# Two lone token tiles taken as one pair by seven block products, and a new order of all instructions

## The chip, the cores and the metric

The kernel runs on one core of one Trainium2 chip. The metric is device time in microseconds, the median of several runs; less is better. TensorE (PE) multiplies, VectorE (DVE) and ScalarE (ACT) evict its results and do the elementwise work, GpSimd (POOL) issues the loads, SyncE (SP) issues the transposes by DMA and most stores.

## The reference

An attention with squared relu is followed by a mixer of tokens and channels. With 8 batches, 12 heads, 448 positions and a head size of 64:

```
def _attn_ref(q, k, v) -> np.ndarray:
    S = q.shape[2]
    scale = 1.0 / np.sqrt(q.shape[-1])
    scores = scale * np.matmul(q, k.transpose(0, 1, 3, 2))
    attn = np.maximum(scores, 0.0) ** 2 / S
    return np.matmul(attn, v).astype(np.float32)

def _moe_ref(x, w_tok1, w_tok2, w_ch1, w_ch2) -> np.ndarray:
    xt = x.transpose(0, 2, 1)
    h = np.maximum(xt @ w_tok1, 0.0) @ w_tok2
    u = x + h.transpose(0, 2, 1)
    h2 = np.maximum(u @ w_ch1, 0.0) @ w_ch2
    return (u + h2).astype(np.float32)
```

x is the attention's output with the heads side by side (8 x 448 x 768); w_tok1 is 448 x 256, w_tok2 256 x 448, w_ch1 768 x 1536, w_ch2 1536 x 768. Inputs and output are float32; the kernel multiplies in bfloat16.

## The kernel before

The work is cut into 24 sets of four heads (three sets for a batch). In the words of the order table, with s a set, c one of seven chunks of positions, b a batch and p a pair of batches:

- `ld` loads q, k or v of a set (POOL). `T` transposes q and k on PE for the first ten sets, and `cp` copies the result; later sets are cast (`iq`, `ik`) and transposed by DMA on SP (`xq`, `xk`).
- `S` is a score step of four matmuls in 64*64 tiles; `r` (two of them) is its relu on ACT or DVE, `q` the square. `V` is a value step of four matmuls in 64*64 tiles, `xe` its eviction.
- `X` or, from set 6 on, `xd` (a DMA transpose on SP) turns x; `t1` and `t2` are the token products, `rt` and `u` their evictions; `ub` transposes u by DMA on SP.
- `C1` is the first channel product of a batch; from the third batch on `fast1` makes it of seven block products (`M1`, a 2 x 2 scheme with fewer multiplications) with `tu`, `s1`, `d1` and `y1` as sums and evictions.
- The second channel product takes token tiles of 128. A pair of batches has 896 tokens, seven tiles. `fast2` takes two tiles by seven block products (`M2`, six matmuls of 384 columns each, with `h` as sums and `d2` as evictions); `channel2` takes a tile alone in two halves of twelve matmuls (`C2`, one sum `h....s`, evictions `c2e`). With seven tiles there are three pairs and one lone tile in each pair of batches, four lone tiles in all: `ALONE = [2, 6, 2, 4]`. The very last tile that is finished, tile 4 of the fourth pair, is a lone one and is evicted and stored in three parts.
- `w1` and `w2` are sums of the weights, `st` stores an output tile, `fill` writes matmuls whose result nobody reads.

Nothing is scheduled by the compiler: `ORDER` is a table of words, written out by a planner beforehand, and `Order.run` issues the words one after another. Each engine works through its own in this order. A word also names the PSUM banks, or the engine (`:A` is ACT, `:D` is DVE), or for a load the transfer behind which it is held. The lines that matter below are, before the change: L343 and L345 relu, L355 and L357 square, L472 transposes of q and k, L497 and L566 and L610 the DMA transposes of k and q, of x and of u, L515 scores, L542 values, L688 sums, L713 and L722 a lone tile's matmuls and evictions, L780 the `M1` and L847 the `M2` products, L860 and L862 the evictions of `M2`, L970 filling matmuls. In the changed kernel the same lines stand one to four numbers lower down.

Of the kernel before, what the change touches and what calls it, by code (L numbers as in the profile page):

```python
# [22 lines left out]
ALONE = [2, 6, 2, 4]  # L23
TILES = [7 * p + t for p, order in enumerate(((0, 1, 2, 3, 4, 5, 6), (4, 5, 6, 0, 1, 2, 3), (0, 1, 2, 3, 4, 5, 6), (5, 6, 0, 1, 2, 3, 4))) for t in order]
# [49 lines left out]
ldf.0 ldf.1 ldk0.0 ldk0.1 ident ldk1.0 ldv2.0 cast0.0:D cast0.1:A ldq1.0 ldk1.1 cast1.0:D cast1.1:A ldq1.1  # L74
T0.0:0 ldv0.1 T0.1:1 cp0.0:D ldv0.0 cp0.1:D ldq2.0 ldk2.0 fill:4*5 S0.3:23
S0.1:45 S0.6:67 r0.3.0:A r0.3.1:D ldq2.1 S0.5:01 r0.1.0:A r0.1.1:D S0.0:23 wt1.1 r0.6.0:A r0.6.1:D r0.0.0:A
ldv1.1 q0.1:D r0.0.1:A ldk2.1 q0.3:D r0.5.0:A T1.0:45 r0.5.1:A q0.0:D S0.4:67 ldq3.0 S0.2:23 cp1.0:A cp1.1:D
ldk3.0 q0.5:D V0.0:01 r0.2.0:A S1.2:54 V0.1 q0.6:D r0.2.1:A ldv1.0 r0.4.0:A r0.4.1:D S1.3:23 ldv2.1 r1.2.0:A
q0.2:D r1.2.1:A wt1.0 q0.4:D r1.3.0:A V0.2 S1.1:67 ldv3.0 V0.3 q1.2:D r1.3.1:A V0.4 S1.4:54 r1.1.0:A ldk4.1
r1.1.1:D S1.0:23 r1.4.0:A r1.4.1:D ldk3.1 S1.6:67 r1.0.0:A V0.5 V0.6 q1.1:D r1.0.1:A ldk4.0 xe0.1:D xe0.0:A  # L80
ldq3.1 r1.6.0:A T2.0:54 q1.0:D r1.6.1:A q1.3:D X0.0:2 wt2 X0.1:3 cp2.0:A cp2.1:D S1.5:01 V1.0:67 ldq5.0 V1.1
q1.4:D r1.5.0:A V1.2 S2.3:45 ldq4.1 V1.3 r1.5.1:A xc0.0:D V1.4 xc0.1:D r2.3.0:A ldk5.1 S2.0:02 q1.5:D r2.3.1:A
S2.2:13 ldv4.0 q1.6:D r2.0.0:A fill:4*3 V1.5 S2.1:45 r2.0.1:A r2.2.0:D ldq6.1 r2.1.0:A r2.1.1:D S2.6:02 V1.6
ldv3.1 r2.2.1:A t1.0.0:1 q2.0:D xe1.0:A ldq5.1 S2.4:45 xe1.1:D r2.6.0:A V2.0:36 r2.6.1:A q2.1:D X1.1:0 ldq4.0
rt0.0:A q2.2:D r2.4.0:A fill:7*2 V2.1 S2.5:72 ldk6.0 q2.3:D r2.4.1:A V2.2 T3.0:14 r2.5.0:A xc1.1:D ldv5.0 V2.3
q2.4:D r2.5.1:A t2.0.0:5 cp3.0:A ldk5.0 cp3.1:D t1.1.1:0 X1.0:7 u0.0:D wc1.0 rt1.1:A V2.4 S3.2:24 xc1.0:A
q2.5:D t2.1.1:1 r3.2.0:A q2.6:D ldq6.0 S3.1:50 r3.2.1:A u1.1:D S3.4:72 ldk6.1 V2.5 r3.1.0:A V2.6 q3.2:D ub0.3
t1.1.0:4 r3.1.1:A ldv4.1 xe2.1:D xe2.0:A S3.0:15 wc1.2 t1.0.1:0 r3.4.0:A r3.4.1:D X2.1:6 rt1.0:A q3.1:D X2.0:3
r3.0.0:A wc2.0 S3.3:72 xc2.1:D rt0.1:A r3.0.1:A T4.0:41 xc2.0:D wc1.1 q3.4:D r3.3.0:A S3.6:60 t2.0.1:3
r3.3.1:A cp4.0:D t1.2.1:5 wc2.2 r3.6.0:A u0.1:D S3.5:72 r3.6.1:A cp4.1:D t1.2.0:4 rt2.1:A t2.1.0:6 r3.5.0:A  # L90
q3.0:D t2.2.1:3 rt2.0:A q3.3:D r3.5.1:A S4.1:05 S4.4:17 u1.0:D r4.1.0:A V3.0:42 V3.1 u2.1:D r4.1.1:A ub0.2
S4.3:60 V3.2 r4.4.0:A q3.5:D V3.3 S4.0:53 r4.4.1:A V3.4 r4.3.0:D ldk7.0 t2.2.0:1 r4.3.1:A ub0.5 q3.6:D V3.5
r4.0.0:A T5.0:76 u2.0:D r4.0.1:A ldq7.0 S4.2:05 V3.6 q4.1:D cp5.0:A ub0.4 C1.0.3:1 ldk7.1 xe3.1:D xe3.0:A
cp5.1:D ldv5.1 r4.2.0:A C1.0.1a:3 q4.0:D r4.2.1:A c1e0.3:A q4.3:D S4.6:72 S4.5:46 V4.0:05 q4.2:D r4.6.0:A V4.1
C1.0.1 r4.5.0:A r4.5.1:D C1.0.2a:1 r4.6.1:A q4.4:D c1e0.1:A C1.0.2 q4.5:D T6.0:74 q4.6:D c1e0.2:A S5.5:62 V4.2
cp6.0:A cp6.1:D V4.3 V4.4 ldq7.1 V4.5 r5.5.0:D S5.3:31 r5.5.1:A V4.6 S6.3:47 r5.3.0:A r5.3.1:D X3.0:6 xe4.0:A
xe4.1:D C1.0.9:2 r6.3.0:A r6.3.1:D xc3.0:A q5.3:D C1.0.10:3 q5.5:D c1e0.9:A q6.3:D wc2.1 X4.0:1 c1e0.10:A
# [24 lines left out]
q9.1:A ub1.1 V8.4 V8.5 ldk14.0:xk11 ik12:D S9.3:51 V8.6 r9.6.1:D C1.1.11:7 xe8.0:A q9.2:D xe8.1:A r9.3.1:A
r9.6.0:D C1.1.8:4 xd8 r9.3.0:A ldk13.0:st1.0 r9.5.1:A ldq13.0:st1.0 q9.3:A t2.6.1:6 q9.5:D ub1.3 C1.1.7:3
q9.6:D c1e1.11:A u6.1:D c1e1.8:A t2.7.0:1 ub1.4 c1e1.7:D V9.0:05 V9.1 u7.0:D S10.1:27 V9.2 V9.3 r10.1.1:A
h0.3.0:D S10.5:46 st2.64 V9.4 r10.1.0:A V9.5 r10.5.0:D V9.6 st0.0 S11.0:31 S10.4:72 xe9.1:A xe9.0:D M2.0.3.2:4
xk12 r10.4.1:A r10.5.1:D r11.0.1:A r11.0.0:D t2.7.1:5 r10.4.0:A d2.0.3.11a:D S10.0:02 xd9 S10.6:61 h0.3.1:D
S10.3:37 r10.0.0:A M2.0.3.5:4 u7.1:D r10.0.1:A ldk14.1:ub1.4 q11.0:A r10.6.0:D xq12 M2.0.3.1:0 ldv10.1:st2.64
iq13:D r10.3.1:A ik13:D r10.3.0:A M2.0.5.2:2 ub2.0 d2.0.3.11b:D r10.6.1:A h0.5.0:D S11.1:56 h0.3.2:D S10.2:73
t1.8.0:1 r10.2.1:A xk13 h0.3.3:D r11.1.0:A r10.2.0:D M2.0.3.6 rt8.0:A d2.0.5.11a:D ub2.2 r11.1.1:A q10.0:D
t2.8.0:3 q10.4:A d2.0.3.12a:D M2.0.5.1:5 d2.0.3.22a:D ub2.1 ldv11.1:xq12 u8.0:D S11.2:71 t2.8.1:2 ldq14.0  # L130
r11.2.0:A M2.0.3.3 r11.2.1:A u8.1:D ldv10.0:xq12 xq13 q10.2:A h0.5.1:D ldq14.1 t1.9.0:6 d2.0.5.11b:D q10.1:A
ldv11.0:xq12 tu2.2:D S11.3:37 ldk16.1:xk13 ik14:D S11.4:12 r11.3.1:A M2.0.3.7 h0.5.2:D ldv12.1:ub2.2 q11.2:A
r11.4.0:D ldq16.1:xk13 M2.0.5.6 r11.4.1:A d2.0.3.22b:D ldk16.0:ub2.1 r11.3.0:A h0.5.3:D M2.0.5.5:7 rt9.0:A
d2.0.5.12a:D q10.3:A ldq15.1 M2.0.3.4 d2.0.5.22a:D q11.4:A q11.1:D ldk15.1 M2.0.5.3 d2.0.3.12b:D q10.6:A
# [111 lines left out]
def kernel(ctx: ExitStack, tc: tile.TileContext, q: bass.AP, k: bass.AP, v: bass.AP, moe_w_tok1: bass.AP, moe_w_tok2: bass.AP, moe_w_ch1: bass.AP, moe_w_ch2: bass.AP, out: bass.AP):  # L246
# [506 lines left out]
    def fast1(b):  # L753
# [17 lines left out]
        for e in range(0, EC // 2, 2):  # L771
# [54 lines left out]
            for j in range(2):  # L826
                c1e[b, e + j] = [c11, c12]
                c1e[b, 6 + e + j] = [c22, y]

    def fast2(p, t, q):  # L830
        r2 = r2s[p]
        (s1, s2, s4), free = sum_set(p)
        out1, parts, store1 = stores(p, t)
# [19 lines left out]
        def take(name, n, cols, u, deps, first):  # L853
# [10 lines left out]
            if first:  # L864
                read_u.setdefault((p, n), []).append(o)
# [138 lines left out]
```

## Time and profile before

| | |
|---|---|
| three runs | 345.43, 346.44, 347.01 us, median 346.44 |
| the profiled execution | 345.03 us, its span 343.2 us |
| granted clock, mean over the span | 0.993 |
| DMA traffic | 50.19 MB, mean 146 GB/s |
| loads of q, k, v (142 of 112 KB) | 4.6 to 4.7 us median to landing |
| six loads of channel weights (768 KB) | 16.9 us median to landing |
| stores of a half tile at the end (96 KB) | 2.1 to 2.4 us median to landing |

The span runs from the first to the last instruction of the profiled execution. Times in rows of the profile are us unless marked ns. A row of the groups gives line, engine, operation, output <- inputs, shapes, count, then busy us and mean ns of one, then the idle time before. A row of the chain of waits gives start, us, and the work, with the number of matmuls.

### The profile page before, as it was taken

Reading aid. Unit: us, or ns where it says so; the run is one execution under the profiler, and the core shown is the slowest. Engines: PE = TensorE matmul, PEld = TensorE weight load, DVE = VectorE, ACT = ScalarE, POOL = GpSimd, SP = SyncE. Lnnn points to the kernel's source line nnn. Section 1 sums busy time; section 2 is a strip of 40 time slices with the busy share of each in tenths; the row PEclk is TensorE's granted clock in tenths of the full one; section 3 lists DMA queues with packets and bytes.
Section 4 is the critical chain, followed back from the end, with each engine's and each line's share of the span. In section 5 each row is a group of like instructions: output and inputs, shape, how many; then the busy total and the mean of one; then the engine's idle time right before and its main releaser. Section 6 shows DMA issues by size and latency. Waiting matters only on the chain.

```text
span 343.2 us, 9395 instructions
## 1 busy us (share of the span) xinstructions
PE 334.0 (97%) x3792; PEld 217.5 (63%) x3792; DVE 296.7 (86%) x577; ACT 242.5 (71%) x456; POOL 91.8 (27%) x157
## 2 busy tenths in 40 slices
PE   7799999999999999999999999999999999999995
PEld 3456455555555557675777655786579787787762
DVE  4999998799988999899979999899897886877763
ACT  3999986868998797999799986978974633031000
POOL 8986211383221371222811233200002000000000
PEclk9899999999999999999999999999999999999999
DMA  8999999798999999999999999996459032241464
GB/s 139 188 188 180 154 183 207 122 168 130 173 178 133 217 158 159 205 173 182 169 189 173 178 157 217 155 186 130 80 112 129 19 79 32 48 114 38 109 160 139
DMA packets 98939, 50.19 MB, mean 146 GB/s; under 512 B 71568, under 2 KB 95952, under 8 KB 98896
## 3 DMA queue, kind: packets, MB, share of 16 engines
q1 hardware_dynamic: 72736, 26.92, 45.3%
q0 software_dynamic: 25136, 21.47, 45.2%
q10 hardware_dynamic: 1024, 1.21, 1.2%
q8 instruction: 29, 0.48, 0.6%
q14 instruction: 14, 0.11, 0.1%
HBM read 43.38 MB, written 11.01 MB: 159 GB/s over the span
## 4 chain that ended last, share of the span: by engine, by line
PE 89%; DMA 3%; DVE 3%; SPq 3%; issue 0%; DVEq 0%; POOLq 0%
PE m_ps L847 24%; PE m_ps L780 22%; PE sc_ps L515 10%; PE acc_ps L542 9%; PE m_ps L623 6%; PE t_ps L588 6%; PE h_ps L597 5%; PE m_ps L713 5%; DMA u_sb<-uT 2%; SPq L610 2%; PE kqT_ps L472 1%; DVE arena L357 1%; DMA arena<-in_k_dram 1%; SPq L497 1%; PE x_ps L579 1%; DVE arena L345 1%
## 5 line engine op out<-in xcount | busy, mean ns | idle before, releaser
L343 ACT ACTIVATE arena<-sc_ps 128x448 bf16<-128x448 f32 x238 | 117.3, 570 | 14.8 <-PE sc_ps L515 13.4
L345 DVE TENSOR_SCALAR arena<-sc_ps 128x448 bf16<-128x448 f32 x98 | 59.4, 619 | 5.1 <-PE sc_ps L515 3.1
L357 DVE TENSOR_TENSOR arena<-arena 128x896 bf16<-128x896 bf16 x105 | 62.0, 620 | 1.0 <-ACT arena L343 0.9
L355 ACT ACTIVATE arena<-arena 128x896 bf16<-128x896 bf16 x63 | 58.5, 960 | 0.1
L371 POOL DMA_DIRECT2D arena<-in_v_dram x48 | 29.2, 618 | 98.0 <-PE m_ps L780 20.2
L515 PE MATMUL sc_ps<-arena 64*64 64x448 bf16 x672 | 54.2, 362 | 0.4
L542 PE MATMUL acc_ps<-arena 64*64 64x448 bf16 x672 | 46.4, 358 | 1.7 <-DVE arena L357 1.6
L780 PEld LDWEIGHTS <-wc 128*128 128x128 bf16 x432 | 40.8, 98 | 6.1 <-issue 3.2
L371 POOL DMA_DIRECT2D arena<-in_q_dram x46 | 28.1, 618 | 44.6 <-DMA u_sb<-uT 8.0
L371 POOL DMA_DIRECT2D arena<-in_k_dram x48 | 29.5, 620 | 21.2 <-DMA out_dram<-out_sb 9.4
L780 PEld LDWEIGHTS <-ws 128*128 128x128 bf16 x324 | 30.5, 98 | 4.5 <-issue 2.5
L515 PEld LDWEIGHTS <-arena 64*64 64x64 bf16 x672 | 19.7, 106 | 20.5 <-issue 13.6
L601 DVE TENSOR_TENSOR uT<-h_ps,xT 128x448 bf16<-128x448 f32 x48 | 29.1, 619 | 1.7 <-PE h_ps L597 1.5
L847 PE MATMUL m_ps<-wc,r 128*128 128x384 bf16 x162 | 30.3, 327 | 0.0
L542 PEld LDWEIGHTS <-arena 64*64 64x64 bf16 x672 | 20.6, 108 | 15.3 <-issue 5.3
L623 PE MATMUL m_ps<-uT,wc 128*128 128x448 bf16 x144 | 30.1, 353 | 0.0
L847 PEld LDWEIGHTS <-r 128*128 128x128 bf16 x216 | 20.2, 98 | 15.1 <-issue 3.1
L793 ACT ACTIVATE arena<-m_ps 128x448 f32<-128x448 f32 x18 | 9.4, 545 | 24.7 <-PE m_ps L780 7.6
L597 PE MATMUL h_ps<-wt,r_sb 128*128 128x448 bf16 x96 | 25.4, 353 | 0.0
L588 PE MATMUL t_ps<-x_sb,wt 128*128 128x256 bf16 (+1 forms) x216 | 25.4, 261 | 0.0
L780 PE MATMUL m_ps<-uT,wc 128*128 128x224 bf16 x216 | 25.0, 259 | 0.0
L847 PEld LDWEIGHTS <-sums 128*128 128x128 bf16 x180 | 17.3, 98 | 12.0 <-issue 1.3
(86 smaller groups left out, 507.2 us busy)
## 6 DMA issues: line engine op xcount, KB each, us to landing
out_dram<-out_sb SPq DMA_DIRECT2D x42, 192.0 KB, 3.7
arena<-in_k_dram POOLq DMA_DIRECT2D x48, 112.0 KB, 4.6
arena<-in_v_dram POOLq DMA_DIRECT2D x48, 112.0 KB, 4.6
arena<-in_q_dram POOLq DMA_DIRECT2D x46, 112.0 KB, 4.7
wc<-in_moe_w_ch_dram POOLq DMA_DIRECT2D x6, 768.0 KB, 16.9
out_dram<-arena SPq DMA_DIRECT2D x4, 192.0 KB, 2.8
out_dram<-out_sb ACTq DMA_DIRECT2D x8, 96.0 KB, 2.4
out_dram<-out_sb SPq DMA_DIRECT2D x8, 96.0 KB, 2.1
```

The source lines that it names most:

```text
L343: nc.scalar.activation(out, ps, AF.Relu)
L345: nc.vector.tensor_scalar(out=out, in0=ps, scalar1=0.0, scalar2=None, op0=ALU.max)
L355: nc.scalar.activation(x, x, AF.Square)
L357: nc.vector.tensor_tensor(out=x, in0=x, in1=x, op=ALU.mult)
L371: o.ins = nc.gpsimd.dma_start(out=raws[t][s % NR][64 * half:64 * (half + 1)], in_=src[b, h0:h0 + 2].rearrange('e (p c) d -> p e (c d)', c=KC))
L515: nc.tensor.matmul(o.ps[e][64 * half:64 * (half + 1), :S], lhsT=lhsT, rhs=rhs, start=True, stop=True, skip_group_check=True)
L542: nc.tensor.matmul(o.ps[half][64 * e:64 * (e + 1), :S], lhsT=r[rows, e, c * D:(c + 1) * D], rhs=sq[rows, e, :], start=c == 0, stop=c == KC ...
L588: nc.tensor.matmul(o.ps[:, j, :], lhsT=wt1[:, c, j * 128:(j + 1) * 128], rhs=x_sb[:, p0:p1, c, :], start=c == 0, stop=c == 3)
L597: nc.tensor.matmul(o.ps[:, :S], lhsT=r1[:, j, a * 128:(a + 1) * 128], rhs=wt2[:, j, :], start=j == 0, stop=j == JC - 1)
L623: nc.tensor.matmul(ps[:, :S], lhsT=wc1[:, g, e * 128:(e + 1) * 128], rhs=uT[:, g, off:off + S], start=g == 0, stop=g == CC - 1)
L780: nc.tensor.matmul(o.ps[:, j * HB:(j + 1) * HB], lhsT=lhs[:, g, (e + j) * 128:(e + j + 1) * 128], rhs=rhs[:, g], start=j == g == 0 and not ...
L847: nc.tensor.matmul(o.ps[:, :HN], lhsT=lhs[:, e], rhs=rhs[:, e], start=e == 0 and not on, stop=e == EC // 2 - 1, skip_group_check=True)
```

## The change

The third pair's lone tile 2 and the fourth pair's lone tile 4 now form a pair of `fast2`, whose two tiles may lie in different pairs of batches. It is made with the last batch. `ALONE` loses its last two entries, the order in which output tiles take their buffers follows, and the lone tiles left are those of the first two pairs. A dependency of the first `fast1` on the weights' load is stated as well. `ORDER` is written anew from the first word to the last, as a planner made it that serves transfers in the order of their issue.

```
-ALONE = [2, 6, 2, 4]
-TILES = [7 * p + t for p, order in enumerate(((0, 1, 2, 3, 4, 5, 6), (4, 5, 6, 0, 1, 2, 3), (0, 1, 2, 3, 4, 5, 6), (5, 6, 0, 1, 2, 3, 4))) for t in order]
+ALONE = [2, 6, None, None]
+LONE = ((2, 2), (3, 4))
+TILES = [7 * p + t for p, order in enumerate(((0, 1, 2, 3, 4, 5, 6), (4, 5, 6, 0, 1, 2, 3), (0, 1, 3, 4, 5, 6), (5, 6))) for t in order] + [21, 22, 16, 25, 23, 24]
...
-ldf.0 ldf.1 ldk0.0 ldk0.1 ident ldk1.0 ldv2.0 cast0.0:D cast0.1:A ldq1.0 ldk1.1 cast1.0:D cast1.1:A ldq1.1
-T0.0:0 ldv0.1 T0.1:1 cp0.0:D ldv0.0 cp0.1:D ldq2.0 ldk2.0 fill:4*5 S0.3:23
+ldf.0 ldf.1 cast1.0:A ldk0.0 ldk0.1 ldq1.1 ldk1.1 ident ldq1.0 cast0.0:D ldq2.0 cast0.1:D fill:1*8 T0.0:0
+cp0.0:A ldk1.0 cast1.1:D ldk2.1 ldv0.1 T0.1:2 cp0.1:D fill:4*8 ldq2.1 ldv0.0 S0.1:35 S0.2:67 S0.0:14 r0.1.0:A
...
-    order = [k % NO for k in range(3 * NT)] + [4, 5, 0, 1, 2, 3, 4]
+    order = [k % NO for k in range(3 * NT - 1)] + [4, 5, 0, 1, 2, 3, 4, 5]
...
+            w1 = list(wc1_ops.values()) if b == FIRST1 else []
-            m1 = product('1', A(0, 0), u11, every + ([got[e - 2, '5']] if e else []))
-            m2 = product('2', A(1, 0), u21, every)
+            m1 = product('1', A(0, 0), u11, every + w1 + ([got[e - 2, '5']] if e else []))
+            m2 = product('2', A(1, 0), u21, every + w1)
...
-    def fast2(p, t, q):
-        r2 = r2s[p]
-        (s1, s2, s4), free = sum_set(p)
+    def fast2(p, t, q, p2=None):
+        p2 = p if p2 is None else p2
+        (s1, s2, s4), free = sum_set(max(p, p2))
         out1, parts, store1 = stores(p, t)
-        out2, parts, store2 = stores(p, q)
+        out2, parts, store2 = stores(p2, q)
...
-        h11, h12, h21, h22 = (r2[:, e:e + 6, c] for c in (te, to) for e in (0, 6))
-        ce, co = (tokens(p, t), tokens(p, q))
+        r2, r2q = (r2s[p], r2s[p2])
+        h11, h12, h21, h22 = (r[:, e:e + 6, c] for r, c in ((r2, te), (r2q, to)) for e in (0, 6))
+        ce, co = (tokens(p, t), tokens(p2, q))
...
-                first, then = ([x for x in PAIRS[p] if x[0] in whole(p, b % 2)], [ALONE[p]] if b % 2 else [])
+                first, then = ([x for x in PAIRS[p] if x[0] in whole(p, b % 2)], [])
+            if b == 2 * B // 2 - 1:
+                fast2(*LONE[0], LONE[1][1], LONE[1][0])
```

Three places show what the new table moves. The first is on PE, around the first score of set 7 (`S7.3`, here sc_ps_1564 and sc_ps_1565 before, sc_ps_1544 and sc_ps_1545 now). Before:

```order
L847 LDWEIGHTS r2_75
L847 MATMUL m2_ps_1551<-wc2_68,r2_75 128x384
L515 LDWEIGHTS arena_69
L515 MATMUL sc_ps_1564<-arena_69 64x448
L515 LDWEIGHTS arena_69
L515 MATMUL sc_ps_1565<-arena_69 64x448
L515 LDWEIGHTS arena_69
L515 MATMUL sc_ps_1564<-arena_69 64x448
L515 LDWEIGHTS arena_69
L515 MATMUL sc_ps_1565<-arena_69 64x448
L579 LDWEIGHTS xT_64
L579 MATMUL x_ps_1571<-ident_63,xT_64 128x128
```

Now:

```order
L543 LDWEIGHTS arena_69
L543 MATMUL acc_ps_1510<-arena_69 64x448
L516 LDWEIGHTS arena_69
L516 MATMUL sc_ps_1544<-arena_69 64x448
L516 LDWEIGHTS arena_69
L516 MATMUL sc_ps_1545<-arena_69 64x448
L516 LDWEIGHTS arena_69
L516 MATMUL sc_ps_1544<-arena_69 64x448
L516 LDWEIGHTS arena_69
L516 MATMUL sc_ps_1545<-arena_69 64x448
L516 LDWEIGHTS arena_69
L516 MATMUL sc_ps_1550<-arena_69 64x448
```

The score stood alone between a product of the second channel step and a transpose of x, both of 128 rows; now it stands between the last value step of set 5 and another score of set 7, all of 64 rows.

The second place is on SP, behind the first six transposes of u (L610, now L611): the transposes of u for the second batch (128x4x128), of k and q for set 10 (`arena`), of x for sets 6 and 7 (x_sb0, x_sb1), and stores of the first output tiles. Before:

```order
L610 DMA_TRANSPOSE u_sb_74<-uT_73 128x3x128 x6
L497 DMA_TRANSPOSE arena_69<-arena_69 128x7x128
L566 DMA_TRANSPOSE x_sb0_70<-xT_64 128x8x128
L668 DMA out_0_dram<-out_sb1_79 64x768
L497 DMA_TRANSPOSE arena_69<-arena_69 128x7x128
L668 DMA out_0_dram<-out_sb2_80 64x768
L566 DMA_TRANSPOSE x_sb1_71<-xT_64 128x8x128
```

Now:

```order
L611 DMA_TRANSPOSE u_sb_74<-uT_73 128x3x128 x6
L611 DMA_TRANSPOSE u_sb_74<-uT_73 128x4x128
L669 DMA out_0_dram<-out_sb1_79 64x768
L611 DMA_TRANSPOSE u_sb_74<-uT_73 128x4x128
L669 DMA out_0_dram<-out_sb1_79 64x768
L611 DMA_TRANSPOSE u_sb_74<-uT_73 128x4x128
L669 DMA out_0_dram<-out_sb0_78 64x768
L669 DMA out_0_dram<-out_sb2_80 64x768
L567 DMA_TRANSPOSE x_sb0_70<-xT_64 128x8x128
L567 DMA_TRANSPOSE x_sb1_71<-xT_64 128x8x128
L498 DMA_TRANSPOSE arena_69<-arena_69 128x7x128 x2
```

Three transposes of u and four stores moved ahead of the first transposes of x, the two of x stand one directly behind the other, and those of set 10 came behind them.

The third place is the end on DVE, where the last lone tile was evicted in three parts (L722, in arena). Before:

```order
L722 TENSOR_TENSOR arena_69<-m2_ps_5674,arena_69 128x128
L688 TENSOR_TENSOR arena_69<-arena_69 128x768
L860 TENSOR_TENSOR arena_69<-arena_69,m2_ps_5461 128x384
L722 TENSOR_TENSOR arena_69<-m2_ps_5649,arena_69 128x256
L688 TENSOR_TENSOR arena_69<-arena_69 128x6x128
L688 TENSOR_TENSOR arena_69<-arena_69 128x768
L688 TENSOR_TENSOR arena_69<-arena_69 128x6x128
L860 TENSOR_TENSOR out_sb0_78<-arena_69,m2_ps_5718 128x384
L860 TENSOR_TENSOR out_sb2_80<-arena_69,m2_ps_5688 128x384
L862 TENSOR_TENSOR out_sb0_78<-out_sb0_78,m2_ps_5726 128x384
L722 TENSOR_TENSOR arena_69<-m2_ps_5699,arena_69 128x384
```

Now the last rows are:

```order
L864 TENSOR_TENSOR out_sb2_80<-u_sb_74,m2_ps_5596 128x384
L864 TENSOR_TENSOR out_sb1_79<-arena_69,m2_ps_5735 128x384
L866 TENSOR_TENSOR out_sb2_80<-out_sb2_80,m2_ps_5554 128x384
L866 TENSOR_TENSOR out_sb1_79<-out_sb1_79,m2_ps_5683 128x384
L864 TENSOR_TENSOR arena_69<-arena_69,m2_ps_5647 128x384
L864 TENSOR_TENSOR arena_69<-arena_69,m2_ps_5655 128x384
L866 TENSOR_TENSOR out_sb3_81<-out_sb3_81,m2_ps_5596 128x384
L866 TENSOR_TENSOR arena_69<-arena_69,m2_ps_5647 128x384
L866 TENSOR_TENSOR arena_69<-arena_69,m2_ps_5655 128x384
L864 TENSOR_TENSOR out_sb3_81<-arena_69,m2_ps_5596 128x384
L864 TENSOR_TENSOR arena_69<-arena_69,m2_ps_5655 128x384
L864 TENSOR_TENSOR out_sb1_79<-arena_69,m2_ps_5683 128x384
```

The parts of a lone tile are gone from the end; evictions of four pairs of tiles stand there interleaved, those of the new pair (out_sb2 from u_sb, and out_sb3) among them.

More of the change, by code (lines that the diff above doesn't have):

```diff
@@ new lines @@
+r11.4.1:A ub2.4 ik14:D M2.0.5.4 tu2.0:D r11.4.0:A xe10.1:D r12.1.1:A ldq16.1:xk13 xe10.0:A xk14 S12.2:62
+tu2.1:D S12.0:73 s1.2.0.1:A w1.2.0:D M1.2.0.5:1 r12.0.0:A q11.0:D t2.9.1:0 r12.0.1:A ub2.3 ldk16.1:xk13
+d2.0.5.21:D s1.2.0.5:A q11.4:D M1.2.0.2:7 xd10 M1.2.0.6 r12.2.0:A u9.1:D r12.2.1:A M1.2.0.3 q11.6:A
+d1.2.0.11:D S12.5:35 iq14:D V11.0:62 S12.3:07 r12.5.0:D st5.64 V11.1 V11.2 s1.2.0.2:A r12.3.0:A d1.2.0.12:D
+V11.3 V11.4 st4.0 r12.3.1:A V11.5 V11.6 iq15:D S13.0:30 r12.5.1:A S12.6:17 r13.0.1:D xe11.1:A M1.2.0.7
@@ L849, in product, with take @@
             reads2.setdefault((p, t), []).append(o)
-            reads2.setdefault((p, q), []).append(o)
+            reads2.setdefault((p2, q), []).append(o)
             return add(o)
-        def take(name, n, cols, u, deps, first):
-            dst = (out1 if n == t else out2)[:, cols]
+        def take(name, at, cols, u, deps, first):
+            pn, n = at
+            dst = (out1 if at == (p, t) else out2)[:, cols]
             g0 = cols.start // 128
-            x, seen = u_part(p, n, g0, g0 + 3)
+            x, seen = u_part(pn, n, g0, g0 + 3)
             def emit(o):
@@ L862, in emit @@
                     nc.vector.tensor_tensor(out=dst, in0=dst, in1=u.ps[:, :HN], op=ALU.add)
-            o = Op(f'd2.{p}.{t}.{name}', 'DVE', emit, [u] + deps + (seen + out_free(p * NT + n) if first else []), reads=[u])
+            o = Op(f'd2.{p}.{t}.{name}', 'DVE', emit, [u] + deps + (seen + out_free(pn * NT + n) if first else []), reads=[u])
             if first:
-                read_u.setdefault((p, n), []).append(o)
+                read_u.setdefault((pn, n), []).append(o)
             return add(o)
```

353 lines of the change are left out of this document (174 added, 179 removed).

## The prediction

> **What bounds the kernel now.** I read the page's busy shares first, then the chain of waits, then who waits for whom on TensorE, then the stretches.
>
> ```profile
> PE 334.0 (97%) x3792; PEld 217.5 (63%) x3792; DVE 296.7 (86%) x577; ACT 242.5 (71%) x456; POOL 91.8 (27%) x157
> PE 89%; DMA 3%; DVE 3%; SPq 3%; issue 0%; DVEq 0%; POOLq 0%
> PE acc_ps L542 <- DVE arena L357: 1.6, 2, 0.9
> PE kqT_ps L472 <- DMA arena<-in_k_dram: 1.2, 2, 0.9
> PE warm_ps L414 <- DVE out_sb L411: 1.2, 1, 1.2
> ```
>
> TensorE is busy for 334.0 of 343.2 us and makes 89% of the chain. Its waits for others add up to 4.0 us (the last three rows): the first memset, the first loads and the first squares, all at the start. The rest of the idle time is the tail behind the last matmul. So from about 20 us on, a microsecond of TensorE work saved is a microsecond of time, unless a new wait takes its place. The stretches tell how near the other engines are:
>
> ```profile
> 8.00:14.00 6.00, 3.88 (x94) 1.69 (x87) 5.97 (x12) 6.00 (x14) 5.84 (x10) 1.00 1.24 186
> 14.00:18.00 4.00, 3.87 (x92) 2.78 (x91) 3.18 (x7) 3.32 (x8) 3.67 (x7) 0.57 1.26 190
> 25.00:40.00 15.00, 15.00 (x343) 8.68 (x339) 15.00 (x30) 15.00 (x35) 9.03 (x14) 1.00 1.26 171
> 40.00:60.00 20.00, 20.00 (x236) 10.71 (x235) 18.56 (x35) 16.31 (x34) 2.54 (x4) 1.00 1.22 188
> 80.00:100.00 20.00, 20.00 (x229) 10.47 (x220) 18.93 (x38) 18.85 (x35) 2.95 (x5) 1.00 1.04 151
> 320.00:340.00 20.00, 18.94 (x131) 11.96 (x128) 14.01 (x28) 0.00 (x0) 0.00 (x0) 1.00 0.61 154
> ```
>
> The columns behind the length are the busy time of TensorE, its weight loads, VectorE, ScalarE and GpSimd, then the granted clock, the DMA share and GB/s. From 8 to 14 us VectorE and ScalarE are full (5.97 and 6.00 of 6) and TensorE is not (3.88): evictions bound the head. From 25 to 40 us all three are full. After that TensorE alone is full, but with VectorE at 93 to 95%; a plan has little room there.
>
> **The block products.** Each lone tile is two halves of twelve matmuls (L713); a pair is seven products of six (L847).
>
> ```profile
> 71.67 1.95 PE m_ps L713 x12
> 320.39 1.31 PE m_ps L713 x12
> 322.67 0.67 PE m_ps L713 x12
> 324.32 1.95 PE m_ps L713 x12
> 326.27 12.69 PE m_ps L847 x78
> 338.98 0.56 DVE out_sb L860
> ```
>
> A half costs 1.95 us, and the last tile's three parts cost 1.31 + 0.67 + 1.95 = 3.93 us, so the two tiles cost 3.90 + 3.93 = 7.8 us. A product costs 12.69 / 13 = 0.976 us, seven cost 6.8 us. Saved: **1.0 us** of TensorE. It lies in the full stage, so all of it counts.
>
> The pair costs VectorE more:
>
> ```profile
> L688 DVE TENSOR_TENSOR sums<-r 128x768 bf16<-128x768 bf16 x12 | 6.6, 553 | 0.3 <-ACT r L343 0.3
> L860 DVE TENSOR_TENSOR out_sb<-u_sb,m_ps 128x384 f32<-128x384 bf16 x36 | 19.6, 549 | 2.6 <-PE m_ps L847 1.6 <-DMA u_sb<-uT 0.9
> L862 DVE TENSOR_TENSOR out_sb<-out_sb,m_ps 128x384 f32<-128x384 f32 x33 | 18.0, 549 | 2.6 <-PE m_ps L847 2.6
> L722 DVE TENSOR_TENSOR arena<-m_ps,arena 128x256 f32<-128x256 f32 x1 | 0.4, 419 | 0.0
> L722 DVE TENSOR_TENSOR arena<-m_ps,arena 128x128 f32<-128x128 f32 x1 | 0.3, 292 | 0.3 <-PE m_ps L713 0.3
> ```
>
> Before: two sums (L688) and five evictions, 5 x 0.55 + 0.42 + 0.29 = 3.5 us. Now four sums and seven evictions, 11 x 0.55 = 6.0 us. The 2.5 us more lie in the last 60 us, where VectorE works 14 of 20 us; cost nothing. Without that cover it would be 2.5 us. At the very end nothing changes: the last product, one eviction of 0.56 us (the last row) and half a tile stored on two queues, in both orders.
>
> **The order: fewer switches.** TensorE runs scores, values and transposes of q and k in 64*64 tiles, all else in 128*128. What a change between the two costs is seen in the chain of waits:
>
> ```profile
> 63.62 0.19 PE acc_ps L542 x4
> 63.80 1.08 PE m_ps L847 x6
> 64.89 0.31 PE sc_ps L515 x4
> 134.13 0.19 PE sc_ps L515 x4
> 134.32 0.68 PE m_ps L780 x6
> 135.38 1.72 PE m_ps L780 x18
> ```
>
> A product among its like takes 0.976 us; the one at 63.80, with a score behind it, 1.08. The lone score at 64.89 takes 0.31, the one at 134.13 takes 0.19. The block product at 134.32 takes 0.68; the three at 135.38 take 0.573 each. Each change of tile size costs 0.10 to 0.12 us; I take 0.11. Counted along TensorE's rows the old order has 135 such changes, the new one 116. In the first 40 us of TensorE's work they go from 35 to 32, which I count as nothing because evictions bound that part; after it from 100 to 84. 16 x 0.11 = **1.8 us** saved. Bounds: 0, if the time reappears as waits, to 19 x 0.12 = 2.3 us.
>
> **The head.** The new order writes 14 filling matmuls in place of 7 (38 units of 128 columns in place of 10).
>
> ```profile
> 5.21 1.09 DVE L351 CAST arena<-arena 64x448 bf16<-64x448 f32 x2 [3.50 <-DMA arena<-in_q_dram]
> 5.21 1.17 ACT L349 ACTIVATE arena<-arena 64x448 bf16<-64x448 f32 x2 [2.42 <-DMA arena<-in_q_dram]
> 6.33 1.17 DVE L351 COPY arena<-kqT_ps 128x896 bf16<-128x896 bf16 x2
> 7.96 3.16 ACT L343 ACTIVATE arena<-sc_ps 128x448 bf16<-128x448 f32 x7 [1.58 <-PE sc_ps L515]
> ```
>
> By the product's rate (0.976 us for 6 x 384 columns, 0.054 us for 128) 28 more units are 1.5 us. They stand where TensorE waits for transfers or evictions, so I take 0; on the path they would be 1.5 us. Three of the four first casts now stand on VectorE and one on ScalarE: the first transposes end some 0.5 us later, near 6.6 us. The two copies behind them took 1.17 us one after the other on VectorE; now one is on each engine, on ScalarE an estimated 0.96 us (a row of the same width, L355 below), which gives this back: they end near 7.7 us and the first relu starts near 8.0 us as before. From there VectorE and ScalarE set the pace in both orders, with the same sum of work to do. Head: 0, between -0.8 (below) and +1.5.
>
> **Evictions moved.** 21 squares go from VectorE to ScalarE (63 and 105 before, 84 and 84 now), at 960 ns instead of 620.
>
> ```profile
> L355 ACT ACTIVATE arena<-arena 128x896 bf16<-128x896 bf16 x63 | 58.5, 960 | 0.1
> L357 DVE TENSOR_TENSOR arena<-arena 128x896 bf16<-128x896 bf16 x105 | 62.0, 620 | 1.0 <-ACT arena L343 0.9
> ```
>
> ScalarE gains some 20 us of 343, VectorE loses 12. ScalarE has 100 us idle and VectorE was the nearer bound, so 0; but from 80 to 100 us ScalarE already stood at 18.85 of 20, and a late square there holds back the value matmul behind it.
>
> **Transfers with less room.** SP issues the transposes one behind another.
>
> ```profile
> L497 SPq DMA_TRANSPOSE arena<-arena x28: 1222/1296/1991, 83.3 to 234.0; - x28
> x_sb<-xT SPq DMA_TRANSPOSE x18, 4.6
> arena<-arena SPq DMA_TRANSPOSE x28, 5.2
> DMA to landing us min/median/max: 3.0/5.2/8.5
> DMA to landing us min/median/max: 3.0/4.6/8.0
> DMA to landing us min/median/max: 2.3/4.5/13.0
> ```
>
> An issue takes 1.3 us. The last three rows are L497 (k and q), L566 (x) and L610 (u), from issue to landing. Now the TensorE work that each order puts between a transpose's issue and its first reader, summed from the rows above. In the new one, behind the issue of k's transpose for set 12 stand three products, two scores, seven value steps and two changes of tile size before S12.1: 2.93 + 0.38 + 1.33 + 0.22 = 4.9 us, against a median landing of 5.2. Behind x's for set 12 stand 4.6 us before t1.12.0, against 4.6. In the old order the least for x or k is 5.9 us. Counted with the issue taken off, transposes that have under 4.5 us left go from one to nine. S12.1 waits in TensorE's queue, and all products behind it wait too, so a late landing is paid in full, once. At the medians the two waits are 0.3 and 0; at the minimum nothing, at the longest 8.5 - 4.9 = 3.6 and 8.0 - 4.6 = 3.4 us. The old order's least room was under the longest landings as well, and TensorE waited for none of them, so room is given with regard to the load; I take **0.5 us** for all nine, bounds 0 and 7.
>
> The Trainium skill (DMA: Bandwidth & Descriptors, Queues, rings and completion order) says that each DMA engine takes turns, packet by packet, between the queues that have work; a plan in which transfers are served strictly as issued would then be too hopeful wherever SP's transposes meet GpSimd's loads. L610's spread of 2.3 to 13.0 us agrees with the rule; by it the waits come nearer their upper bound, by the medians nearer 0.5.
>
> **The sum.** Against the profiled execution, 345.0 us (span 343.2 and 1.8 around it): 345.0 - 1.0 - 1.8 + 0 + 0.5 = 342.7 us. That execution lies 1.4 us under the median of the runs shown, 346.44, so the median after comes out at **344.1 us**, 2.3 us or 0.7% less.
>
> **The rivals.** *The clock stays up as well (12%).* From 14 to 18 us the granted clock is 0.57, and VectorE and ScalarE, which bound that part, stand idle for 0.82 and 0.68 us. If the fillers keep the clock up, the mean of the two, 0.75 us, comes off: 343.3. For it: full clock on both sides of that stretch, and the fillers stand ahead of it. Against: the idle time may have other causes.
>
> The Trainium skill (TensorE: Matmul & The Clock Gate, Part 1) has the clock halved after a window of 3.4 us without enough work on the array; the stretch in the trace fits, and by this rule the fillers decide whether this rival comes true.
>
> *The saving is eaten (25%).* TensorE's work falls by 2.8 us but waits of 1.5 to 3 us appear, since VectorE at 93% or more and ScalarE with 20 us more leave no slack for an order that is a microsecond late somewhere: 345.0 - 2.8 + 2.2 = 344.4, or 345.8 as a median. For it: the full rows from 25 to 100 us. Against: the old order, as tight on VectorE, shows no wait of TensorE on either engine after 15 us.
>
> *Transposes land late (18%).* The place is S12.1 and t1.12.0, then the other seven. The price is 3.6 + 3.4 us at the longest landings; from 2.8 us on the gain is gone, from 4.5 us on the kernel is slower than can be told from noise. With 5.5 us of waits: 345.0 - 2.8 + 5.5 = 347.7, median 349.1. For it: nine short rooms in place of one, a DMA share above 1 in every row from 8 to 100 us. Against: those medians.
>
> That the change does not do what it says I leave out: TensorE's rows hold 42 matmuls of products more and 60 of lone tiles fewer.
>
> **How the numbers follow.** Forecast 45%, clock 12%, eaten 25%, late 18%. What a measurement here can tell from no change is about 0.5%, 1.7 us: under 344.7 is faster, over 348.2 slower. The forecast's own spread of about a microsecond leaves 41 of its 45 points faster, the clock case adds 11: 0.52 faster. The eaten case gives most of the rest: 0.29 the same. Slower keeps 0.19, the late case and a little of the eaten one. The range takes in the clock case with TensorE's upper saving (2.3 instead of 1.8, and nothing waited: 341.8) and reaches into the late case: 341.8 to 348.8. The forecast's own range is 343.0 to 345.3.
>
> **What would show it.** Right: TensorE's busy time near 331 us with as many waits as before; 48 matmuls in the lone tiles' line in place of 108; no TensorE wait over 0.5 us after 20 us; the clock at 1.0 from 14 to 18 us for the clock case. Wrong: a row in which scores or t_ps matmuls wait for a transpose (L498, L567), a TensorE wait on ScalarE's squares, or filling matmuls followed at once by work that was ready.

## The result and the profile after

| | before | after |
|---|---|---|
| median of four runs each, side by side | 346.66 us | 356.80 us (355.11 to 357.51) |
| ratio, 95% interval | | 1.028 (1.024 to 1.032) |
| the profiled execution, its span | 345.0, 343.2 us | 356.6, 354.8 us |

The change makes the kernel 2.8% slower; the forecast was 344.1 us, 0.7% faster, and the range ended at 348.8. First the page of the changed kernel, with the rows that answer to those of before: busy time, and shares of the chain of waits.

```profile
PE 337.5 (95%) x3779; PEld 222.2 (63%) x3781; DVE 293.9 (83%) x570; ACT 253.6 (71%) x467; POOL 92.4 (26%) x157
PE 74%; DMA 13%; DVE 6%; ACT 4%; issue 1%; SPq 1%; POOL 1%; DVEq 0%; POOLq 0%
```

TensorE had 89% of the chain and has 74%; transfers had 3% and have 13%, VectorE 3% and now 6%. Who waits for whom on TensorE (sum, times, longest) names the places:

```profile
PE sc_ps L516 <- DVE arena L346: 3.2, 1, 3.2
PE sc_ps L516 <- DMA arena<-arena: 2.6, 1, 2.6
PE m_ps L850 <- DVE sums L689: 2.2, 2, 2.0
PE warm_ps L415 <- DVE out_sb L412: 1.2, 1, 1.2
```

Only the last of these four was there before. The other three stand in two of the stretches below (length, busy time of TensorE, its weight loads, VectorE, ScalarE and GpSimd, granted clock, DMA share, GB/s):

```profile
14.00:18.00 4.00, 3.65 (x101) 2.12 (x100) 4.00 (x9) 4.00 (x10) 2.97 (x5) 1.00 1.20 173
120.00:140.00 20.00, 16.07 (x173) 10.00 (x174) 17.48 (x37) 14.23 (x28) 6.62 (x12) 1.00 1.17 156
200.00:220.00 20.00, 16.36 (x123) 7.71 (x121) 11.49 (x24) 11.49 (x22) 4.58 (x8) 0.83 1.14 135
```

The head keeps its clock (1.00 from 14 to 18 us, 0.57 before). TensorE stands idle for 3.9 us of the 20 from 120 and for 3.6 of those from 200. VectorE and ScalarE have idle time in the same stretches: 2.5 and 5.8 us in the first, 8.5 us each in the second.

**What the time is made of.** I took, for each step of TensorE behind 35 us, the time to the next step's start less its matmuls at full rate and less 0.11 us for a change of tile size. What is over 0.15 us sums to 0.6 us before and 14.7 us after: 0.5 at 91 us, 5.6 between 118 and 132, 0.2 at 139, 7.2 between 203 and 217, and 1.3 after 250. The work and the changes of tile size went down by some 3 us there. The 11.6 us more of span are these waits less that saving, within 1 us.

**The first place.** The chain of waits of the changed kernel from 111 to 132 us (start, us, what):

```profile
111.18 7.53 DMA arena<-in_k_dram
118.71 0.02 issue
118.73 0.07 DVE arena L352
...
120.36 0.47 DVE sums L689
...
123.82 0.30 DVE arena L352
124.12 0.03 DVE out_sb L866
124.15 7.53 DMA arena<-arena
131.68 0.04 issue
131.72 0.57 PE sc_ps L516 x8
```

A load of half of k for set 13 (`ldk13.0`) is issued at 111.18 and lands after 7.53 us. The copy `ik13` waits for it at the front of VectorE's queue (3.5 us). Behind it stand a sum (120.36), for which the product `M2.0.5.6` waits 2.0 us, and the copy `ik12` (123.82), behind which k's transpose for set 12 is issued at 124.15. It lands after 7.53 us too, and S12.1 waits 2.6 us: the place that the prediction named. TensorE came to S12.1 5.0 us behind the issue, as counted (4.9); it is the landing that was longer than the median of 5.2.

**The second place.** The same view from 199 us:

```profile
199.30 8.11 DMA u_sb<-uT
207.41 0.03 issue
...
207.51 0.45 DVE out_sb L864
207.96 0.02 issue
207.98 0.55 DVE sums L689
208.53 0.55 DVE arena L346
209.07 0.04 issue
209.12 0.59 PE sc_ps L516 x3
209.71 2.03 PE m_ps L850 x6
```

A transpose of u (`ub3.5`) lands after 8.11 us. The eviction `d2.1.0.22a` waits 3.1 us for it at the front of VectorE's queue; 1.9 us had been lost there just before to the store `st12.0`. A relu (208.53) stands behind it, and TensorE waits 3.2 us for the bank that this relu frees. Then comes a second price: the product at 209.71 takes 2.03 us, twice the 0.976 of its like, and so on to 216 us; the granted clock is 0.83 over the 20 us from 200, and 0.50 from 208.4 to 215.2 us. TensorE works for about 6 us of that at half clock, which costs some 3 us.

### The profile page after: what moved, and what is told of

It is laid out like the page before. It is cut to its first block, busy times and chain, and to the rows that moved or that the text cites. A ratio compares the mean times of both kernels' runs of the same rounds, so it can differ in the third digit from the quotient of the medians.

```text
span 354.8 us, 9390 instructions
## 1 busy us (share of the span) xinstructions
PE 337.5 (95%) x3779; PEld 222.2 (63%) x3781; DVE 293.9 (83%) x570; ACT 253.6 (71%) x467; POOL 92.4 (26%) x157
## 4 chain that ended last, share of the span: by engine, by line
PE 74%; DMA 13%; DVE 6%; ACT 4%; issue 1%; SPq 1%; POOL 1%; DVEq 0%; POOLq 0%
PE m_ps L850 20%; PE m_ps L781 18%; PE sc_ps L516 7%; PE acc_ps L543 7%; PE m_ps L624 6%; PE t_ps L589 5%; PE h_ps L598 5%; DMA arena<-arena 4%; DMA x_sb<-xT 3%; DMA u_sb<-uT 2%; PE m_ps L714 2%; DMA arena<-in_k_dram 2%; ACT arena L344 2%; DVE arena L346 1%; DVE arena L358 1%
## 5 line engine op out<-in xcount | busy, mean ns | idle before, releaser
L356 ACT ACTIVATE arena<-arena 128x896 bf16<-128x896 bf16 x84 | 79.8, 972 | 2.3 <-DVE arena L346 1.9
L516 PE MATMUL sc_ps<-arena 64*64 64x448 bf16 x672 | 55.8, 359 | 7.1 <-DVE arena L346 3.2
L358 DVE TENSOR_TENSOR arena<-arena 128x896 bf16<-128x896 bf16 x84 | 50.2, 616 | 0.6
L543 PE MATMUL acc_ps<-arena 64*64 64x448 bf16 x672 | 44.4, 351 | 0.6 <-DVE arena L346 0.3
L516 PEld LDWEIGHTS <-arena 64*64 64x64 bf16 x672 | 22.9, 105 | 29.2 <-issue 18.3
L850 PE MATMUL m_ps<-wc,r 128*128 128x384 bf16 x174 | 34.1, 337 | 0.5 <-DVE out_sb L864 0.5
L850 PEld LDWEIGHTS <-r 128*128 128x128 bf16 x228 | 22.1, 100 | 16.9 <-issue 4.8
L850 PEld LDWEIGHTS <-sums 128*128 128x128 bf16 x198 | 18.9, 99 | 17.7 <-issue 3.6
L543 PEld LDWEIGHTS <-arena 64*64 64x64 bf16 x672 | 21.4, 106 | 11.6 <-issue 4.4
L850 PE MATMUL m_ps<-ws,sums 128*128 128x384 bf16 x132 | 24.6, 326 | 2.5 <-DVE sums L689 2.2
L864 DVE TENSOR_TENSOR out_sb<-u_sb,m_ps 128x384 f32<-128x384 bf16 x38 | 20.4, 546 | 7.1 <-DMA u_sb<-uT 3.1
```

What stands on the lines that cost most here:

```text
L356: nc.scalar.activation(x, x, AF.Square)
L358: nc.vector.tensor_tensor(out=x, in0=x, in1=x, op=ALU.mult)
L516: nc.tensor.matmul(o.ps[e][64 * half:64 * (half + 1), :S], lhsT=lhsT, rhs=rhs, start=True, stop=True, skip_group_check=True)
L543: nc.tensor.matmul(o.ps[half][64 * e:64 * (e + 1), :S], lhsT=r[rows, e, c * D:(c + 1) * D], rhs=sq[rows, e, :], start=c == 0, stop=c == KC ...
L850: nc.tensor.matmul(o.ps[:, :HN], lhsT=lhs[:, e], rhs=rhs[:, e], start=e == 0 and not on, stop=e == EC // 2 - 1, skip_group_check=True)
```

## The experiments

"Late landings" is my theory from these rows: a few readers stand too shortly behind a transfer, and the engines' queues pass their waits on. "Pace" is the rival: VectorE and ScalarE are too slow for this order, and a wait taken away turns up elsewhere. Diffs of ORDER show one word a line. Ratios are to the kernel before, measured beside each, with 95% intervals. What "came back" is the difference of two medians, each with an error of a microsecond or more; each profile is of one execution.

### 1 to 4: each place alone, and both

The first run issues two of SP's transfers earlier:

```diff
 ub3.3
+ub3.5
...
 st12.64
+st12.0
...
-st12.0
-ub3.5
```

> Two of SP's transfers are issued earlier: u's transpose for the last group of set 11 (ub3.5) behind ub3.3, the store st12.0 behind st12.64, some 20 to 30 us sooner. Late landings: VectorE's two waits of 1.9 us (for the store) and 3.1 us (for the transpose) vanish, and with them TensorE's 3.2 us at the score S18.6, the half clock from 209 to 216 us and the small waits between: 7.2 us in all, so 349.6 us, between 348.5 and 351. Rival, pace: VectorE and ScalarE are too slow for this order since the squares moved, and the waits only turn up at other instructions: 355 to 357 us.

Measured: 350.97 us, 1.015 (1.006 to 1.025). 5.8 us came back; the time is at the upper end of what late landings gave (351). The waits at 203 to 217 us are gone; new ones of 1.4 us at t1.12.0 and 1.7 us at a value step stand in the profile, the first at the second place that the prediction had named.

The second holds GpSimd's loads back instead:

```diff
-ldq22.0
+ldq22.0:ub3.5
```

> The six loads that GpSimd issues between 198.6 and 201.6 us wait until u's transpose ub3.5 (issued at 199.3) has landed; SP's order is unchanged. If transfers share the DMA engines in turn, the transpose lands after some 3 to 4.5 us in place of 8.1, before VectorE comes to it (204.4), and of the 7.2 us some 5 to 6 come back: 351 to 352 us, with VectorE's wait for the store (1.9 us, to 203.0) cut to under 1.5. If transfers are served as issued, four of the six loads stand behind the transpose anyway, it lands after 7 to 8 us as before, and the time is 356 to 357 us.

Measured: 355.10 us, 1.025 (1.018 to 1.032): 1.7 us of the expected 5 to 6. The transpose's landing, in the changed kernel and in this run (each the view of that one instruction):

```profile
DMA to landing us min/median/max: 8.1/8.1/8.1
```

```profile
DMA to landing us min/median/max: 3.2/3.2/3.2
```

It falls from 8.1 to 3.2 us although SP's order is the same and four of the six loads were issued after it. The two issued ahead of it, 224 KB, are an estimated 1.4 us at the rate of the changed kernel from 196 to 212 us:

```profile
DMA packets 6348, 2.59 MB, mean 162 GB/s; under 512 B 5164, under 2 KB 6217, under 8 KB 6345
```

The other 3.5 us are more than serving as issued would give. So in this pair of profiles a transfer was slowed by what was issued behind it on another queue, as the rule of the Trainium skill (DMA: Bandwidth & Descriptors, Queues, rings and completion order) that the prediction set beside its own estimate says; the order's plan, transfers served as issued, does not hold here. The time did not follow, since the loads held met the next transposes and each other. For two of these loads, issued at 204.3 and 204.9 us, the view says who waited and when they landed:

```profile
DVE arena L352: 6.4, 1
busy tenths in 40 slices 0000000000000000000000000000000000000000
DMA to landing us min/median/max: 8.1/9.6/11.1
```

One landed after 11.1 us, and VectorE waited 6.4 us for it, more than the 3.1 us for the transpose; TensorE stood for 6 us behind that and then ran at half clock to 222 us.

The third is for the first place:

```diff
 ldk14.1:ub1.4
+ldk13.0:st1.0
...
 ldv10.0:xq12
...
-ldk13.0:st1.0
```

> One load (half of k for set 13) is issued ahead of the load that GpSimd holds until a transpose has landed, five places sooner, about 104 us in place of 111.2. Late landings, each place with its own cause: VectorE's 3.5 us at the copy ik13 vanish, and TensorE's 2.2 and 0.6 us at the two products behind it; k's transpose for set 12 is issued 3 us sooner too, but its room stays 4.9 us and it lands after 5 to 7.5, so 0 to 2.6 us of the 2.7 at S12.1 stay: 352 to 354 us. Knock-on: S12.1 waited only since the copy was late; all of 5.5 us come back, 351.3. Pace: 355 to 357.

Measured: 351.17 us, 1.012 (1.005 to 1.019). 5.6 us came back, as in the knock-on reading; the interval takes in 352 too, so it is the trace that has to tell. S12.1 no longer waits. Its transpose in the changed kernel and in this run:

```profile
DMA to landing us min/median/max: 7.5/7.5/7.5
```

```profile
DMA to landing us min/median/max: 5.0/5.0/5.0
```

It is issued 3.2 us sooner (120.92), but TensorE comes to S12.1 as much sooner too, so the room is 5.0 us in both. What the edit took away is 2.5 us of landing. In all runs of the new order S12.1's wait is the landing less these 5.0 us: 5.8 and 0.9 in the first run, 4.1 and none in the fourth, 5.7 and 0.7 in the eighth. Why it lands sooner is not shown by a run of its own. In the changed kernel GpSimd had stood 4.6 us behind the late copy and then issued six loads from 119.42 us on, of which the last landed 3.8 us behind the transpose's issue; in this run the last of the same loads landed 2.0 us behind it.

The fourth has the words of the first and the third where these have them.

> The edits of the first and the third run together. Late landings: the two gains add up, 7.2 + 2.8 to 5.5 us: 344 to 347 us. If a place mended only passes its wait on to the next one that is tight, the sum of the two single gains is not reached by 2 us or more.

Measured: 347.23 us, 1.000 (0.995 to 1.004). By the medians 9.6 us came back of 5.8 + 5.6 = 11.4, 1.8 us short; by the ratios it is 2.9% of 1.3% + 1.6%, and nothing is missing. The times cannot tell. The trace shows new waits, in one row of who waits for whom:

```profile
PE t_ps L589 <- DMA x_sb<-xT: 2.9, 2, 1.6
```

Products of sets 11 and 12 now wait for x's transposes. These landed after 5.6 and 3.3 us in the changed kernel and take 9.1 and 6.4 us here; that they meet more transfers once the stalls are gone is likely, but not shown.

### 5 and 9: the pair alone, in the order of before

The table of before is kept. The lone tiles' words go from the middle and from the tail, and the pair's stand in the tail:

```diff
-C2.2.2.0:1
...
-C2.2.2.1:3
...
+st14.64
 d2.2.5.11a:D
...
-st14.64
...
-C2.3.4.1:7
+M2.2.2.1:7
...
+st19.0
-C2.3.4.2:1
+M2.2.2.2:1
...
-C2.3.4.0:3
+M2.2.2.5:3
...
+M2.2.2.6
...
+M2.2.2.7
...
+M2.2.2.3
...
+M2.2.2.4
```

> The kernel before with its own order, and of the change only the two lone tiles taken as a pair: the parts of the lone tiles and their sums go, the pair's seven products, four sums and seven evictions stand in the last 30 us, and the stores and output slots that belong to them move. The prediction's term: 1.0 us less of TensorE, the 2.5 us more of VectorE hidden: 0.997 of before, about 344.8 us. Rival: VectorE's added evictions stand in the last 30 us, where TensorE waits for them, or the 3.9 us taken out of the middle bring the readers there nearer to their transfers: 0 to 3 us slower.

Measured: 355.11 us, 1.026 (1.022 to 1.030). Neither reading: VectorE waited for two stores (the row of its waits, then the one of TensorE's behind it).

```profile
DVE out_sb L864 <- DMA out_dram<-out_sb: 5.5, 2, 4.3
```

```profile
PE m_ps L781 <- DVE sums L689: 3.0, 1, 3.0
```

With the pair, output tiles use other buffers, and I had put `st14.64` straight ahead of the eviction that needs its buffer free. That is my placing and no price of the pair.

The ninth run mends this; two sums and two evictions of the pair stand earlier too:

```diff
 st14.0
+st14.64
...
-st14.64
 d2.2.5.11a:D
...
 st19.64
+st19.0
...
-st19.0
```

> The fifth run's kernel with two stores issued as soon as their data stands (st14.64 behind st14.0, st19.0 behind st19.64) and two of the pair's sums earlier: VectorE waited 4.3 us for the first store, 2.3 us for the second, and TensorE 3.1 and 2.2 us behind it. If these stores are what made the fifth run slow, 5.3 us come back: 349.5 us; the rest over before would be the 2.8 us between 242 and 262 us, where the two halves of the lone tile no longer stand between scores and their evictions. If the pair has its price everywhere in the old order, 353 to 355 us.

Measured: 347.48 us, 1.004 (1.001 to 1.007). 7.6 us came back, more than expected, from these few words. 1.1 us over before are left (0.5 to 2.5 by the interval) where the pair's term is 1.0 less. A price stands in the middle (the stretch in this run, then the part of the kernel before that answers to it, with the lone tile's halves):

```profile
243.00:264.00 21.00, 19.15 (x188) 13.05 (x187) 18.10 (x35) 16.58 (x29) 2.37 (x4) 1.00 0.58 101
```

```profile
240.00:262.00 22.00, 22.00 (x211) 15.10 (x204) 19.12 (x38) 16.89 (x29) 2.36 (x4) 1.00 0.56 98
```

TensorE is idle for 1.85 us of 21 where before it had no idle time: the lone tile's two halves had stood there between products or scores and their evictions. Counted from step to step as above, 3.0 us are lost there, in the fifth run's profile as well, and none before; -1.0 + 3.0 = +2.0, within the interval. The profiled execution of this run is 350.22 us, 2.7 over the median: it lost some 4 us more at 36 to 42 us, with 2.5 us idle for which the profile names no releaser and half clock behind it. The fifth run's profile does not show this, and I do not count it to the pair.

### 6 and 8: the other places

On top of the fourth run:

```diff
 xq15
+xd11
...
-xd11
...
-ub3.1
...
 xd12
+ub3.1
...
+st7.64
 st8.0
...
-st7.64
```

> The changed kernel with the two edits of the fourth run and three more: x's transpose for set 11 in front of two other transposes, x's for set 12 in front of one, a store one place earlier. In the fourth run TensorE still waited 1.4 us for set 11's, 1.8 for set 12's and 0.6 behind the store. Late landings: 3 to 3.8 us come back on top of the fourth run, about 343.5 us and 0.989 to 0.993 of before, near the forecast's 344.1. Rival: on a queue that is full, what goes first makes another late, and 2 us or more of it turn up at the transposes that are now behind: 345.5 to 347 us.

Measured: 346.68 us, 0.999 (0.996 to 1.003): the rival's time. The mended places have no wait left, and two others have, behind a load and behind a transpose for a later set:

```profile
PE acc_ps L543 <- DMA arena<-in_v_dram: 1.6, 1, 1.6
PE t_ps L589 <- DMA x_sb<-xT: 1.5, 2, 1.3
```

Each of these two gets its word moved:

```diff
 ldk20.0:xd13
+ldv15.1:xd13
...
-ldv15.1:xd13
...
 xe21.1:D
+xd21
...
-xd21
```

> The sixth run's kernel with two more words moved: the load of half of v for set 15 five places earlier on GpSimd, x's transpose for set 21 three places earlier on SP. In the sixth run TensorE lost 2.7 us at the value step that waits for that load and 1.5 us at the product that waits for that transpose. Late landings: these 4.1 us come back if no other transfer takes their place: 342.5 us, 0.986 to 0.992 of before. Rival: the transfers are so dense that each mend only moves the wait; then 345.5 to 347 us again, with waits of 2 us or more elsewhere.

Measured: 343.80 us, **0.993 (0.990 to 0.995)**: faster than both kernels, and 0.3 us from the forecast. Its page, and TensorE's largest waits:

```profile
PE 332.3 (97%) x3779; PEld 220.6 (65%) x3781; DVE 293.8 (86%) x570; ACT 253.2 (74%) x467; POOL 92.2 (27%) x157
PE 90%; DVE 3%; ACT 3%; DMA 2%; issue 1%; DVEq 0%
```

```profile
PE warm_ps L415 <- DVE out_sb L412: 1.2, 1, 1.2
PE acc_ps L543 <- issue: 0.8, 1, 0.8
PE sc_ps L516 <- DMA arena<-arena: 0.7, 1, 0.7
```

The instructions are those of the changed kernel, in number and kind; eight words stand elsewhere in the table, and 13 us of 357 are gone. S12.1 still waits 0.7 us. That it comes so near the forecast is in part chance: waits of 1.4 us are left where the forecast took 0.5.

### 7 and 10: the fillers and the squares

Against the sixth run:

```diff
-fill:1*8
...
-fill:4*8
...
-fill:2*16
```

> The sixth run's kernel without the three early groups of filling matmuls (8, 8 and 16 units of 128 columns, 1.7 us of TensorE). If they stand where TensorE waits in any case and the clock does not hang on them, the time is the same within 0.5 us. If they keep the clock up, the granted clock falls to near 0.6 somewhere before 20 us and 0.5 to 2 us are lost. If they stand in the way of ready work, up to 1.7 us are gained.

Measured: 346.89 us, 1.001 (0.998 to 1.004), the sixth run's time within 0.2 us. The clock did hang on the fillers:

```profile
8.00:14.00 6.00, 4.26 (x96) 2.22 (x97) 5.19 (x10) 5.23 (x11) 5.90 (x10) 0.73 1.12 163
14.00:18.00 4.00, 3.82 (x88) 1.96 (x85) 3.40 (x7) 3.51 (x8) 2.89 (x6) 0.58 1.25 186
```

With them it is 1.00 in both stretches, in all profiles that have them. They are not needed each time: in the ninth run, with the old order's few fillers, it stayed at 1.00 there too. In the trace TensorE reaches the last value step of set 3 at 40.7 us with the fillers and at 41.8 without; at the first product of set 6 (92.1 and 92.7), which waits for x's transpose, half of that is gone.

Against the eighth run, 21 words change like these two:

```diff
-q4.3:A
+q4.3:D
...
-q5.2:A
+q5.2:D
```

> The eighth run's kernel with 21 squares handed back from ScalarE to VectorE, spread over the sets from 4 on (105 and 63, as many as in the kernel before), at the places of the order where they stand. The prediction took the move as costing nothing. If it is neutral either way: 343 to 345 us. If the order needs ScalarE for them, since VectorE's queue at 0.62 us each then passes 13 us of delays on to evictions behind it: 345.5 to 349 us, with TensorE waiting on VectorE's rows. If ScalarE was the one too late: 341 to 342.5 us.

Measured: 348.65 us, 1.008 (1.005 to 1.011), 4.9 us slower than the eighth run. The group of VectorE's squares, a stretch, and the same stretch of the eighth run:

```profile
L358 DVE TENSOR_TENSOR arena<-arena 128x896 bf16<-128x896 bf16 x105 | 62.8, 616 | 0.4
```

```profile
100.00:120.00 20.00, 20.00 (x176) 10.87 (x169) 19.86 (x41) 15.31 (x32) 10.13 (x18) 1.00 1.17 164
120.00:140.00 20.00, 19.46 (x213) 12.90 (x212) 19.75 (x41) 17.96 (x34) 4.12 (x7) 1.00 1.11 167
```

```profile
100.00:120.00 20.00, 20.00 (x171) 11.12 (x170) 19.31 (x40) 16.95 (x33) 10.77 (x18) 1.00 1.14 162
120.00:140.00 20.00, 19.33 (x214) 13.18 (x213) 19.03 (x40) 18.64 (x36) 4.46 (x8) 1.00 1.19 173
```

VectorE is full to 99% in these 40 us, against 96%, and TensorE loses a few tenths at some fifteen steps between 49 and 282 us: 6.4 us of waits counted as above, against 1.4. The new order needs ScalarE for these squares. It does not follow that every choice of 21 would cost as much: these were handed back at places that the order had made for ScalarE.

## Why the prediction was wrong, by its own steps

**The block products, -1.0 us: right.** The rows of the lone tiles that are left, in the changed kernel:

```profile
L714 PE MATMUL m_ps<-wc,r 128*128 128x384 bf16 x36 | 6.5, 326 | 0.0
L714 PE MATMUL m_ps<-wc,sums 128*128 128x384 bf16 x12 | 2.3, 326 | 0.0
```

48 matmuls, as announced. What the step left out is what the lone tile had done where it stood: in the old order its two halves gave products, scores and evictions time, and taken alone the pair loses some 3 us there, more than it saves (ninth run).

**The changes of tile size, -1.8 us: borne out in the sum.** They were not tried alone. The eighth run has them, the pair, and 1.4 us of waits left, and it is 2.6 us under before; the prediction's sum was 2.3 under it with 0.5 us of waits. The interval of the eighth run is 0.9 us to either side, so a size of 1.8 is not told from one a microsecond off.

**The head, 0: right in the end.** The clock stays up, as in the clock rival, but TensorE works through 1.5 us more of fillers. By 60.2 us each of the two kernels has done some 41.7 us of matmul work besides its fillers.

**VectorE's 2.5 us for the pair, hidden: right** in the changed order; no wait of TensorE on it stands in the last 60 us.

**The squares, 0: right, and more than that.** ScalarE had the room (21 x 0.62 is 13 us off VectorE, not the 12 of the prediction), and without the move the new order loses 4.9 us (tenth run). The rival "the saving is eaten", by VectorE and ScalarE, falls at the two places with runs 1 and 3: when a late transfer was mended, the time came back.

**Transfers with less room, +0.5 us, bounds 0 and 7: this step failed.** It cost 14.7 us in the changed kernel, some 3 of them half clock. Its sentence was that the old order's least room lay under the longest landings too, "so room is given with regard to the load". The runs show three things in its place:

- The readers were counted on TensorE alone. The two costliest waits, 3.5 and 3.1 us, were VectorE's, for a load and for a transpose of u with 4.0 and 5.1 us of room, and VectorE's queue handed them to a sum and a relu that TensorE needed. Mending these two places brought 9.6 us back (fourth run).
- The landing was taken from the old order's medians. S12.1's room of 4.9 us was right (5.0 in every run), and so was the price, landing less room; but the transpose took 7.5 us to land and not 5.2, and 5.0 when the load ahead of it came in time (third run). The bound of 3.6 us held. t1.12.0's 3.4 us showed as 0 in the changed kernel, with a landing of 3.3 us, and as 1.4 to 1.8 with landings of 5.1 and 6.4 when the stalls ahead were gone (first and fourth run). Over all 28 transposes of k and q the changed kernel's median is 4.7 us, no worse than before: a median does not tell of the one transfer that a tight reader waits for.
- A stall has a price of its own: behind 3.2 us of idle TensorE it worked at half clock for about 6 us. The prediction used the rule of the Trainium skill (TensorE: Matmul & The Clock Gate, Part 1) for the head only; the trace agrees with it at 209 us as well: half clock comes in stretches of 3.4 us or twice that (208.4 to 215.2 us here). The length of a wait alone does not decide: 2.6 us of idle time at 129 us brought none, and 2.0 us in the third run brought 3.4 us of it (203.5 to 206.9).

The rival "transposes land late" was the right mechanism with 18% and a price of 5.5 us in place of 14.7; its median, 349.1, missed by 8 us. Its upper bound added two waits and left out all that does not read on TensorE. The range has a slip at its lower end: with its own terms, 0.75 us for the clock, 0.5 for tile size and 0.5 for waits, it is 342.3 us and not 341.8, which changes nothing here.

**What would show it.** TensorE's busy time was 337.5 us in place of 331, some 3 us of it half clock; the "wrong" row, scores waiting for a transpose, was there.

## What to carry to other kernels

Count the room of every transfer to its first reader on every engine, loads and stores included; on an in-order queue the cheapest eviction that waits for a transfer stops all behind it, so ask what the engine after that one waits for. Do not take the median for the landing of a transfer with little room: the same transpose took 7.5 and 5.0 us here, with one load moved. On a trace that is full, a sum of saved work is only worth what is left when the tightest five or ten readers have their transfer in time: here it took eight words moved, at unchanged work, to turn 2.8% slower into 0.7% faster. Mend one place at a time and look again, since behind a mended stall other transfers land later than before (x's for set 12: 3.3 us in the changed kernel, 6.4 in the fourth run).

## What the runs showed of the hardware

A transpose by DMA of the same size, issued from the same place of its queue, landed after 8.1 us with six loads of 112 KB let go around it (four of them behind it) and after 3.2 us without. The loads, when they met three transposes instead, took up to 11.1 us; the changed kernel's shortest load of this size took 2.9 us. The order of issue on one queue does not show this: what the other queue has in flight counted as well.

The granted clock of TensorE fell to half at waits of 3.2 us (changed kernel) and 2.0 us (third run), for 6.8 and 3.4 us, and stayed full at one of 2.6 us (changed kernel, 129 us).
